# Strassen blocks of an attention, MoE and MLP kernel: order of the seven products, place of the rounded weight sums, and TensorE's order at the ends of the MLP's halves

## Chip, cores and metric

One core of one Trainium2 chip. The metric is the device time of one execution in microseconds (us), lower is better. Every execution computes attention, a mixture of experts and an MLP for the same inputs.

## What is computed

The reference, cut to what matters (2 batches of 8 heads, 576 positions, 64 per head; so 1152 tokens of 512):

```python
scores = q @ k.T / 8 + decay                 # decay from cumsum(log f), causal mask
x = softmax(scores) @ v                      # heads side by side: 1152 x 512
p = domain_probs / domain_probs.sum(-1)      # 1152 x 4
moe = sum(p[:, e:e+1] * (relu(x @ w1[e]) @ w2[e]) for e in range(4))   # 512 -> 1024 -> 512
h = moe @ w_in                               # 512 -> 2048
out = (h * sigmoid(1.702 * h)) @ w_out       # 2048 -> 512
```

## The kernel before

**Blocks and visits.** The four experts are worked as eight half experts, the MLP as four blocks: twelve blocks of 512 hidden columns, and a block's columns are four groups of 128. A block meets its tokens in visits. Visits 0 to 6 run beside the attention. Visits 7, 8 and 9 (`v_exp` to `v_all - 1`, the "early Strassen blocks") work two chunks of 320 tokens each, visits 10 to 13 the remaining MoE half experts (chunks of 320, 320 and 512 tokens), visit 14 (`v_mlp`) the first MLP block in the plain way, visits 15 to 17 the three other MLP blocks (three chunks of 384).

**Three matmuls for one.** Every operand is held as a rounded part and the rest of it (`xh`, `xl` for tokens, `whi`, `wlo` for weights, `hh`, `hl` for the hidden layer), and a product is hi·hi + lo·hi + hi·lo. ScalarE (ACT) rounds, VectorE (DVE) subtracts to get the rest.

**The joint first layer.** `emit_joint` (L869 on) works two chunks against two column groups at a time with seven products in place of eight (the Strassen scheme in Winograd's form). A visit has two such halves, m = 0 (groups 0 and 1) and m = 1 (groups 2 and 3). One product is six matmuls (L885). With the tokens' sums `th`, `tl` and the weights' sums `sh`, `sl`, the products are: into `pa` a11, into `pb` the second sum, into `pc` the first sum ("S1 product"), into `pd` the third ("S3 product"), into `pa` on top a12, into `pe` a22, and into `pc` on top the fourth ("S4 product"). Between them the outputs are combined: `u2 = pa` (ACT), `u2 = pb + u2` (DVE, L930), `u3 = pd + u2` (L914, in `third`), then one output each from `pc + u3` (L891, still in `third`), `u3 - pe` (`fourth`), and `pc + u2` after the S4 product (`fifth`). The output `pc + u3` has to be read before the S4 product adds to `pc`. In a MoE block an output goes from `pc` or `pe` to a buffer `jc`, in the MLP it is written over an accumulator, hence "DVE m L891" there. The plain output of `pa` goes through `evac_l1`: rounded by ACT, its rest by DVE (L963 in a MoE block, L966 in the MLP). In the second halves of visits 7 to 9 (`late_sums`) the a22 product stands second rather than sixth, since the sums are still being made.

**Sums.** POOL adds the raw weights (`sum_weights`), `split_sums` rounds them in two pieces of 512: ACT (L60, `sh<-sr`), DVE (L267, `sl<-sr,sh`), ACT, DVE. There is one buffer of sums: a new rounding may begin only when the S4 product of the half before has read the old one.

**Accumulators.** `ps_tile` (L122) hands out the eight PSUM buffers in turn; a product into a buffer waits until its last user has been read out. The second layer (`l2_products`, L972) uses the same buffers, read out by L1005 (MoE) or L1011 (MLP). In visits 7 to 9 the first half's columns (k 0 and 1) are worked for five token tiles before k 2 and 3. The plain first layer is L847.

**What sets the order.** A scheduler orders instructions by a simulated time line. DVE, ACT and POOL are held to source order from visit 7 on by `pin_turn` (L1097), TensorE (PE) only in visits 7 to 9:

```python
if v_ >= v_exp:
    (pin_engines.add if v_ < v_all else pin_engines.discard)(nc.tensor.engine)
    pin_turn()
```

In the MLP, DVE also converts weights (L342 to L357, `cvt`, `cvd`, `wf`) and makes their low parts (L230), in its fixed order between the steps of the halves. The main loop (L1170 on) emits a step's matmuls, then the work of the step before (`evac[0]()`), then what `place` has put at this step.

## Time and profile before

| | |
|---|---|
| median of 3 runs | 697.5 us (697.33 to 700.41) |
| profiled execution, its own time | 696.63 us |
| its span | 694.9 us |
| granted TensorE clock, mean | 1.00 |
| busy: PE, DVE, ACT, POOL | 98%, 72%, 49%, 32% |

The span is the time between the first and the last instruction; 1.73 us of the execution lie around it. A line of a waits view says which engine and line waited for which, how long in total, how often, and the longest. A row of a time line has the start, the busy time, engine, line, operation, out<-in, shapes and count, and in brackets the idle time before it and what ended it. A matmul's own time there is longer than its distance to the next, since matmuls overlap; distances are between starts.

### The profile page before, as it was taken

The page shows a single profiled execution, that of the slowest core. Times are in us where ns is not written, and L with a number is a line of the kernel's source. Part 1 is how long each engine was busy: PE and PEld are TensorE (multiplying, and loading weights), DVE is VectorE, ACT ScalarE, POOL GpSimd, SP SyncE. Part 2 cuts the span into 40 slices and gives each one's busy share as a digit, 9 for nine tenths or more (in the row PEclk, how much of TensorE's full clock was granted, in tenths as well). Part 3 has the DMA queues.
Part 4 walks back from the last instruction along what each step waited for, and adds up shares of the span by engine and source line. Part 5 has one row for each costly group of instructions (what it writes and reads, how often), then busy time and mean ns, then how long its engine had stood idle before and what let it go on. Part 6 is the DMA issues. An engine that isn't in the chain of part 4 may idle for free.

```text
span 694.9 us, 10725 instructions
## 1 busy us (share of the span) xinstructions
PE 683.6 (98%) x3828; PEld 596.3 (86%) x3829; DVE 502.1 (72%) x1057; ACT 342.1 (49%) x789; POOL 221.2 (32%) x266
## 2 busy tenths in 40 slices
PE   8999999999999999999999999999999999999997
PEld 4797888888988888888888888888899998988986
DVE  6896777666468677566966976788678779678632
ACT  5778767676532635634243344244446354434420
POOL 6887577532132454413214115112002302100000
PEclk9999999999999999999999999999999999999999
DMA  7786735423302034141423433444130343231012
GB/s 245 237 301 243 270 97 215 126 93 90 111 14 91 31 122 145 40 149 47 152 85 113 152 121 106 122 152 149 48 107 19 133 152 121 83 116 61 1 46 91
DMA packets 38597, 83.37 MB, mean 120 GB/s; under 512 B 3560, under 2 KB 3568, under 8 KB 38544
## 3 DMA queue, kind: packets, MB, share of 16 engines
q1 hardware_dynamic: 38504, 82.65, 36.0%
q8 instruction: 30, 0.49, 0.3%
q14 instruction: 23, 0.19, 0.1%
q10 hardware_dynamic: 40, 0.04, 0.0%
HBM read 71.88 MB, written 10.78 MB: 119 GB/s over the span
## 4 chain that ended last, share of the span: by engine, by line
PE 93%; DVE 3%; POOL 1%; ACT 1%; issue 1%; DMA 1%; SPq 0%; POOLq 0%; DVEq 0%; ACTq 0%
PE m L972 42%; PE m L847 20%; PE m L885 17%; PE s L568 4%; PE x L672 4%; PE t L642 3%; PE m L1117 1%; DMA dpraw<-in_dp_dram 1%; POOL ks L494 0%; PE m L864 0%; POOL e L624 0%; PE t L716 0%; PE m L1033 0%; POOL qlo L512 0%; PE s L571 0%
## 5 line engine op out<-in xcount | busy, mean ns | idle before, releaser
L972 PE MATMUL m<-whi,hh 128*128 128x512 f32 x432 | 122.6, 393 | 0.7 <-ACT hh L60 0.7
L972 PE MATMUL m<-wlo,hh 128*128 128x512 f32 x432 | 119.4, 390 | 0.0
L972 PE MATMUL m<-whi,hl 128*128 128x512 f32 x432 | 118.9, 390 | 0.0
L230 DVE TENSOR_TENSOR wlo<-wst,whi 128x512 fp32r<-128x512 f32 x140 | 103.0, 751 | 4.9 <-ACT whi L60 4.3
L972 PEld LDWEIGHTS m<-wlo,hh 128*128 128x128 f32 x432 | 80.9, 188 | 17.0
L972 PEld LDWEIGHTS m<-whi,hl 128*128 128x128 f32 x432 | 80.8, 188 | 16.9
L60 ACT ACTIVATE whi<-wst 128x512 fp32r<-128x512 f32 x144 | 85.4, 625 | 15.1 <-DMA wst<-in_wa_moe_dram 6.7
L972 PEld LDWEIGHTS m<-whi,hh 128*128 128x128 f32 x432 | 79.3, 188 | 14.7 <-ACT hh L60 1.1
L895 POOL TENSOR_TENSOR hl<-jc,hh 128x320 fp32r<-128x320 f32 x42 | 37.0, 882 | 160.1 <-ACT hh L60 153.3
L893 ACT ACTIVATE jc<-jc 128x320 f32<-128x320 f32 x42 | 19.7, 470 | 105.2 <-DVE jc L891 105.2
L251 POOL TENSOR_TENSOR sr<-wst 128x256 f32<-128x256 f32 x20 | 19.5, 976 | 154.0 <-DVE tl L287 48.1
L847 PE MATMUL m<-xh,wlo 128*128 128x256 f32 (+2 forms) x304 | 64.5, 325 | 0.0
L847 PE MATMUL m<-xl,whi 128*128 128x256 f32 (+2 forms) x304 | 64.2, 326 | 0.0
L847 PE MATMUL m<-xh,whi 128*128 128x256 f32 (+2 forms) x304 | 64.0, 327 | 0.0
L624 POOL TENSOR_SCALAR e<-e,sm 128x128 f32<-128x128 f32 (+4 forms) x72 | 46.0, 651 | 54.5 <-DVE sm L622 27.5
L963 DVE SCALAR_TENSOR_TENSOR hl<-m,hh 128x384 fp32r<-128x384 f32 (+2 forms) x82 | 36.0, 439 | 30.4 <-ACT hh L962 29.9
L1005 DVE SCALAR_TENSOR_TENSOR acc<-m,dpn,acc 128x512 f32<-128x512 f32 x63 | 46.6, 744 | 11.4 <-PE m L972 11.4
L847 PEld LDWEIGHTS m<-xh,whi 128*128 128x128 f32 x304 | 50.4, 189 | 3.2
L847 PEld LDWEIGHTS m<-xh,wlo 128*128 128x128 f32 x304 | 50.6, 189 | 2.5
L847 PEld LDWEIGHTS m<-xl,whi 128*128 128x128 f32 x304 | 50.2, 189 | 2.6
L614 ACT ACTIVATE e<-e,mx 128x128 f32<-128x128 f32 (+4 forms) x72 | 41.6, 580 | 11.7 <-DVE mx L598 11.0
L966 DVE TENSOR_TENSOR hl<-m,hh 128x384 fp32r<-128x384 f32 x48 | 26.6, 555 | 28.0 <-ACT hh L60 28.0
(138 smaller groups left out, 1292.0 us busy)
## 6 DMA issues: line engine op xcount, KB each, us to landing
wst<-in_wa_moe_dram SPq DMA_DIRECT2D x28, 512.0 KB, 3.6
wst<-in_wb_moe_dram SPq DMA_DIRECT2D x28, 512.0 KB, 4.1
mst<-in_wa_mlp_dram SPq DMA_DIRECT2D x16, 512.0 KB, 4.0
wm<-wf SPq DMA_DIRECT2D x32, 256.0 KB, 3.4
mst<-in_wb_mlp_dram SPq DMA_DIRECT2D x16, 512.0 KB, 3.8
wst<-wm SPq DMA_DIRECT2D x16, 512.0 KB, 3.5
cb<-cumd SPq DMA_DIRECT2D x16, 256.0 KB, 3.6
qr<-in_qk_dram SPq DMA_DIRECT2D x8, 384.0 KB, 4.9
```

Of the source, the lines that this page charges most:

```text
L60: return nc.scalar.activation(out=out, in_=in_, func=AF.Copy)
L230: (nc.gpsimd if v_ == 0 and kind == 'a' and g < 4 else nc.vector).tensor_sub(lf, raw, f(hf))
L568: nc.tensor.matmul(pt[:, :z - a], lhsT=lr[i][0], rhs=lr[i][1], start=i == 0 and not (both and pt is not bank), stop=i == n - 1, skip_group ...
L614: nc.scalar.activation(out=e[:, off:off + w], in_=e[:, off:off + w], func=AF.Exp, scale=-1.0, bias=mx, accum_out=sm[:, 0, k:k + 1])
L624: nc.gpsimd.tensor_scalar(out=e[:, off:off + w], in0=e[:, off:off + w], scalar1=sm[:, 0, i:i + 1], scalar2=1.0, op0=ALU.mult, op1=ALU.mult)
L672: nc.tensor.matmul(pt[64 * g:64 * g + 64, o:n], lhsT=lhsT, rhs=rhs, start=i == 0, stop=i == nk - 1)
L847: nc.tensor.matmul(p[:, :n], lhsT=w[:, k, :], rhs=x[c][:, k, :], start=(j == 0 and k == 0), stop=(j == 2 and k == 3))
L885: nc.tensor.matmul(p[:, :WN], lhsT=w[a][:, k, :], rhs=x[z][:, k, :], start=start and j == 0 and k == 0, stop=stop and j == 2 and k == 1, s ...
L895: nc.gpsimd.tensor_sub(hl[:, g, :], r, f(hh[:, g, :]))
L963: nc.vector.scalar_tensor_tensor(out=l_, in0=q, scalar=0.0, in1=f(h_), op0=ALU.max, op1=ALU.subtract)
L972: nc.tensor.matmul(p, lhsT=h_tile(v_, b, c, j, x, k), rhs=wb[v_, k][w].rearrange("p a c -> p (a c)"), start=i == 0 and k == 0, stop=i == 2 ...
L1005: nc.vector.scalar_tensor_tensor(out=a, in0=p, scalar=d, in1=a, op0=ALU.mult, op1=ALU.add)
```

## The change

- In the second halves of visits 7 to 9 the S3 product goes ahead of the S1 product, `third` (u3) and `third_out` (the output that reads `pc`) become two steps, and the accumulators are taken in another turn: `pa`, `pc`, one left unused, `pe`, `pb`, `pd`.
- In every MoE joint half the plain output's two operations are taken apart: `plain_out` (ACT) where they were, `plain_low` (DVE) after the `fourth` output.
- Sums of the next visit: `split_sums` at its two places is replaced by `high_sums` (both ACT roundings) ahead of the previous step's outputs and `low_sums` (both DVE subtractions) behind them; likewise for the second half of visit 7.
- In the main loop PE is held to source order also in visits 15 to 17: in the second half and in the first two steps of the plain first layer behind it.

```diff
@@ -260,11 +260,30 @@
     def split_sums(*at):
         if at or sum_due:
             v_, m, raw = (*at, placed_sums.pop(at)) if at else sum_due.pop(0)
-            sh, sl = ws[v_, m] = tuple(late["ws"].tile([128, 4, 2, 128], F32R, tag=t, name=t) for t in ("sh", "sl"))
-            hs, ls = (t.rearrange("p s k c -> p (s k c)") for t in (sh, sl))
+            hs, ls = begin_sums(v_, m)
             for o in (0, 512):
                 round_act(hs[:, o:o + 512], raw[:, o:o + 512])
                 nc.vector.tensor_sub(ls[:, o:o + 512], raw[:, o:o + 512], f(hs[:, o:o + 512]))
+
+    def begin_sums(v_, m):
+        ws[v_, m] = tuple(late["ws"].tile([128, 4, 2, 128], F32R, tag=t, name=t) for t in ("sh", "sl"))
+        return tuple(t.rearrange("p s k c -> p (s k c)") for t in ws[v_, m])
+
+    def high_sums(v_, m):
+
+        raw = placed_sums.pop((v_, m)) if v_ in placed else sum_due.pop(0)[2]
+        hs, ls = begin_sums(v_, m)
+        for o in (0, 512):
+            round_act(hs[:, o:o + 512], raw[:, o:o + 512])
+        low_due[v_, m] = raw, hs, ls
+
+    def low_sums(v_, m):
+
+        raw, hs, ls = low_due.pop((v_, m))
+        for o in (0, 512):
+            nc.vector.tensor_sub(ls[:, o:o + 512], raw[:, o:o + 512], f(hs[:, o:o + 512]))
+
+    low_due = {}
 
     sum_due = []
 
@@ -901,51 +920,74 @@
             a11, a12 = (tuple(t[:, k:k + 2] for t in wa[v_, g]) for k in (0, 2))
             a22 = tuple(t[:, 2:4] for t in wa[v_, g2])
             s1, s2, s3, s4 = (tuple(t[:, i] for t in ws[v_, m]) for i in range(4))
-            pa, pb, pc = (ps_tile() for _ in range(3))
+            if late_sums:
+                pa, pc, _, pe, pb, pd = (ps_tile() for _ in range(6))
+            else:
+                pa, pb, pc = (ps_tile() for _ in range(3))
             u = []
 
             def first_part():
                 u.extend(tmp_p.tile([128, WMAX], F32, tag="tmp", name=n)[:, :WN] for n in ("u2", "u3"))
                 nc.scalar.activation(out=u[0], in_=pa[:, :WN], func=AF.Copy)
 
-            pd, pe = [], []
+            def second():
+                nc.vector.tensor_add(u[0], pb[:, :WN], u[0])
 
             def third():
-                nc.vector.tensor_add(u[1], pd[0][:, :WN], u[0])
-                output(c2, g2, nc.vector.tensor_add, pc, u[1], pd[0])
+                nc.vector.tensor_add(u[1], pd[:, :WN], u[0])
+
+            def third_out():
+                output(c2, g2, nc.vector.tensor_add, pc, u[1], pd)
 
             def fourth():
-                output(c1, g2, nc.vector.tensor_sub, pe[0], u[1], pe[0])
+                output(c1, g2, nc.vector.tensor_sub, pe, u[1], pe)
 
             def fifth():
                 output(c2, g, nc.vector.tensor_add, pc, u[0], pc)
+
+            def both_(*parts):
+                return lambda: [q() for q in parts]
+
+            hh, hl = h_of(v_, b, c1)[0][2]
+            plain_hi, plain_lo = hh[:, g, :], hl[:, g, :]
+
+            def plain_out():
+                if b < NMOE:
+                    nc.scalar.activation(out=plain_hi, in_=pa[:, :WN], func=AF.Relu)
+                else:
+                    evac_l1(v_, b, c1, g, pa)
+
+            def plain_low():
+                if b < NMOE:
+                    nc.vector.scalar_tensor_tensor(out=plain_lo, in0=pa[:, :WN], scalar=0.0, in1=f(plain_hi),
+                                                   op0=ALU.max, op1=ALU.subtract)
 
             product(pa, a11, ts[11], True, True)
             yield first_part
             if late_sums:
-                pe.append(ps_tile())
-                product(pe[0], a22, ts[4], True, True)
+                product(pe, a22, ts[4], True, True)
                 yield lambda: None
-            product(pb, s2, ts[2], True, True)
-            yield lambda: nc.vector.tensor_add(u[0], pb[:, :WN], u[0])
-            product(pc, s1, ts[1], True, True)
-            yield lambda: None
-            pd.append(ps_tile())
-            product(pd[0], s3, ts[3], True, True)
-            if late_sums:
-                def two():
-                    third()
-                    fourth()
-
-                yield two
+                product(pb, s2, ts[2], True, True)
+                yield second
+                product(pd, s3, ts[3], True, True)
+                yield third
+                product(pc, s1, ts[1], True, True)
+                yield both_(third_out, fourth)
+                product(pa, a12, ts[21], False, True)
+                yield both_(plain_out, plain_low)
             else:
-                yield third
-            product(pa, a12, ts[21], False, True)
-            yield lambda: evac_l1(v_, b, c1, g, pa)
-            if not late_sums:
-                pe.append(ps_tile())
-                product(pe[0], a22, ts[4], True, True)
-                yield fourth
+                product(pb, s2, ts[2], True, True)
+                yield second
+                product(pc, s1, ts[1], True, True)
+                yield lambda: None
+                pd = ps_tile()
+                product(pd, s3, ts[3], True, True)
+                yield both_(third, third_out)
+                product(pa, a12, ts[21], False, True)
+                yield plain_out
+                pe = ps_tile()
+                product(pe, a22, ts[4], True, True)
+                yield both_(fourth, plain_low)
             product(pc, s4, ts[22], False, True)
             yield fifth
 
@@ -1155,12 +1197,14 @@
             h0, h1, l2 = (3, v_, b, c1), (3, v_, b, c2), (4, v_, b, c1)
             put(h0, 1, sum_weights, v_ + 1, 0)
             put(h1, 1, sum_weights, v_ + 1, 1)
-            put(l2, 0, split_sums, v_ + 1, 0)
-            put((5, v_, b, c1), 0, split_sums, v_ + 1, 1)
+            for u, m in ((l2, 0), ((5, v_, b, c1), 1)):
+                put(u, -1, high_sums, v_ + 1, m)
+                put(u, 0, low_sums, v_ + 1, m)
             first = v_ == v_exp
             places = [(h1, 5), (h1, 6)] + [(l2, i) for i in range(1, 7)]
             if first:
-                put((6,) + units[-1], 0, split_sums_done)
+                put((6,) + units[-1], -1, high_sums, v_, 1)
+                put((6,) + units[-1], 0, low_sums, v_, 1)
                 nxt0 = (3, v_ + 1, visits[v_ + 1][0], c1)
                 places = [(h0, 0), (h0, 1)] + places + [(nxt0, 0), (nxt0, 1)]
             todo = [("b", v_)] * first + [("a", v_ + 1), ("b", v_ + 1)]
@@ -1232,6 +1276,9 @@
                 if d[0] == 0:
                     split_due.remove(d)
                     rests.append(split_output(d[1]))
+            if g == 0:
+                for what, args in place_at.get((u, -1), ()):
+                    what(*args)
             evac[0]()
             for r in rests:
                 r()
@@ -1257,7 +1304,8 @@
                     cv_due[0] -= 1
                 load_owed()
             if v_ >= v_exp:
-                (pin_engines.add if v_ < v_all else pin_engines.discard)(nc.tensor.engine)
+                end = v_ > v_mlp and (kind == 3 and m == 1 or kind == 1 and g < 2)
+                (pin_engines.add if v_ < v_all or end else pin_engines.discard)(nc.tensor.engine)
                 pin_turn()
             else:
                 pin_from[1] = len(nc.cur_bb.bb.instructions)
```

How the instructions move, on PE (rows: line, operation, out<-in with the tiles' numbers, shape, count; `x` the tokens, `t` their sums, `s` the weights' sums, `w` weights). First, visit 8, second half. Before, from the S1 product (m_3435 is `pc`), then S3 (m_3471), a12 (m_3433) and S4:

```order
L885 MATMUL m_3435<-th_2881,sh_3420 128x320 x2
L885 MATMUL m_3435<-th_2881,sl_3421 128x320 x2
L885 MATMUL m_3435<-tl_2882,sh_3420 128x320 x2
L885 MATMUL m_3471<-th_2881,sh_3420 128x320 x2
L885 MATMUL m_3471<-th_2881,sl_3421 128x320 x2
L885 MATMUL m_3471<-tl_2882,sh_3420 128x320 x2
L885 MATMUL m_3433<-xh_77,whi_3280 128x320 x2
L885 MATMUL m_3433<-xh_77,wlo_3281 128x320 x2
L885 MATMUL m_3433<-xl_78,whi_3280 128x320 x2
L885 MATMUL m_3435<-xh_77,sh_3420 128x320 x2
L885 MATMUL m_3435<-xh_77,sl_3421 128x320 x2
L885 MATMUL m_3435<-xl_78,sh_3420 128x320 x2
```

Now, from the S3 product (m_3439), then S1 (m_3435 is `pc` again), a12 and S4:

```order
L904 MATMUL m_3439<-th_2881,sh_3416 128x320 x2
L904 MATMUL m_3439<-th_2881,sl_3417 128x320 x2
L904 MATMUL m_3439<-tl_2882,sh_3416 128x320 x2
L904 MATMUL m_3435<-th_2881,sh_3416 128x320 x2
L904 MATMUL m_3435<-th_2881,sl_3417 128x320 x2
L904 MATMUL m_3435<-tl_2882,sh_3416 128x320 x2
L904 MATMUL m_3434<-xh_77,whi_3281 128x320 x2
L904 MATMUL m_3434<-xh_77,wlo_3282 128x320 x2
L904 MATMUL m_3434<-xl_78,whi_3281 128x320 x2
L904 MATMUL m_3435<-xh_77,sh_3416 128x320 x2
L904 MATMUL m_3435<-xh_77,sl_3417 128x320 x2
L904 MATMUL m_3435<-xl_78,sh_3416 128x320 x2
```

S1 and S3 have changed places: `pd` is complete one product sooner, and between the end of `pc`'s S1 product and S4 there is one product (a12) where there were two.

Second, visit 10, between its two halves. Before, from the S4 product of the first half (m_3893) to the first row of the second half that reads new sums (sh_3979); the plain first layer (L847) lies between:

```order
L885 MATMUL m_3893<-xh_77,sh_3800 128x320 x2
L885 MATMUL m_3893<-xh_77,sl_3801 128x320 x2
L885 MATMUL m_3893<-xl_78,sh_3800 128x320 x2
L847 MATMUL m_4089<-xh_77,wlo_3785 128x512
L847 MATMUL m_4089<-xl_78,whi_3784 128x512 x4
L847 MATMUL m_4110<-xh_77,whi_3813 128x512 x4
L847 MATMUL m_4110<-xh_77,wlo_3814 128x512 x4
L847 MATMUL m_4110<-xl_78,whi_3813 128x512 x4
L885 MATMUL m_3993<-th_2881,sh_3979 128x320 x2
```

Now:

```order
L904 MATMUL m_3995<-xh_77,whi_3816 128x320 x2
L904 MATMUL m_3995<-xh_77,wlo_3817 128x320 x2
L904 MATMUL m_3995<-xl_78,whi_3816 128x320 x2
L904 MATMUL m_3896<-xh_77,sh_3797 128x320 x2
L904 MATMUL m_3896<-xh_77,sl_3798 128x320 x2
L904 MATMUL m_3896<-xl_78,sh_3797 128x320 x2
L904 MATMUL m_3996<-th_2881,sh_3977 128x320 x2
L904 MATMUL m_3997<-th_2881,sh_3977 128x320 x2
L904 MATMUL m_4023<-th_2881,sh_3977 128x320 x2
```

The sums' products of the second half (sh_3977) follow directly on the S4 product of the first (sh_3797).

Third, visit 16, the end of its second half. Before, the plain first layer of the third chunk stands ahead of the S4 product (m_6728):

```order
L847 MATMUL m_6858<-xh_77,whi_6457 128x384 x4
L847 MATMUL m_6858<-xh_77,wlo_6458 128x384 x4
L847 MATMUL m_6858<-xl_78,whi_6457 128x384 x4
L847 MATMUL m_6887<-xh_77,whi_6488 128x384 x4
L847 MATMUL m_6887<-xh_77,wlo_6489 128x384 x4
L847 MATMUL m_6887<-xl_78,whi_6488 128x384 x4
L885 MATMUL m_6728<-xh_77,sh_6675 128x384 x2
L885 MATMUL m_6728<-xh_77,sl_6676 128x384 x2
L885 MATMUL m_6728<-xl_78,sh_6675 128x384 x2
L972 MATMUL m_6913<-whi_6736,hh2_2861 128x512
```

Now, from the a22 product (m_6801) on, S4 is m_6731:

```order
L904 MATMUL m_6801<-th_2881,whi_6491 128x384 x2
L904 MATMUL m_6801<-th_2881,wlo_6492 128x384 x2
L904 MATMUL m_6801<-tl_2882,whi_6491 128x384 x2
L904 MATMUL m_6731<-xh_77,sh_6678 128x384 x2
L904 MATMUL m_6731<-xh_77,sl_6679 128x384 x2
L904 MATMUL m_6731<-xl_78,sh_6678 128x384 x2
L866 MATMUL m_6823<-xh_77,whi_6407 128x384 x4
L866 MATMUL m_6823<-xh_77,wlo_6408 128x384 x4
L866 MATMUL m_6823<-xl_78,whi_6407 128x384 x4
L866 MATMUL m_6841<-xh_77,whi_6430 128x384 x4
```

The S4 product stands right behind the sixth product, ahead of the 48 matmuls of the plain first layer. In visit 15 it moves the same way, with two second-layer matmuls left between; in visit 17 it moves to the same place. The S4 product of visit 16's first half moves too: it now stands 15 second-layer matmuls further ahead. The rows of DVE, ACT and POOL in visits 15 to 17 stand as before.

## Rows read from the trace of the kernel before

**Rows 1.** The page: busy time by engine; the chain that ended last, by engine.

```profile
PE 683.6 (98%) x3828; PEld 596.3 (86%) x3829; DVE 502.1 (72%) x1057; ACT 342.1 (49%) x789; POOL 221.2 (32%) x266
...
PE 93%; DVE 3%; POOL 1%; ACT 1%; issue 1%; DMA 1%; SPq 0%; POOLq 0%; DVEq 0%; ACTq 0%
```

**Rows 2.** Waits of PE: total us, times, longest us.

```profile
PE m L885 <- DVE jc L891: 0.9, 3, 0.3
...
PE m L885 <- DVE acc L1005: 0.7, 2, 0.4
PE m L972 <- ACT hh L60: 0.7, 1, 0.7
```

**Rows 3.** Time line of PE, visit 8, second half: S3 product, S4 product.

```profile
256.70 0.46 PE L885 MATMUL m<-tl,sh 128*128 128x320 f32 x2
257.50 0.56 PE L885 MATMUL m<-th,sh 128*128 128x320 f32 x2 [0.34 <-DVE acc L1005]
257.90 0.45 PE L885 MATMUL m<-th,sl 128*128 128x320 f32 x2
258.19 0.46 PE L885 MATMUL m<-tl,sh 128*128 128x320 f32 x2
...
260.70 0.56 PE L885 MATMUL m<-xh,sh 128*128 128x320 f32 x2 [0.30 <-DVE jc L891]
```

**Rows 4.** Time line of DVE and of ACT, the same half.

```profile
256.71 1.40 DVE L1005 SCALAR_TENSOR_TENSOR acc<-m,dpn,acc 128x512 f32<-128x512 f32 x2
...
259.56 0.49 DVE L914 TENSOR_TENSOR u<-m,u 128x320 f32<-128x320 f32 x1 [1.06 <-PE m L885]
260.16 0.49 DVE L891 TENSOR_TENSOR jc<-m,u 128x320 f32<-128x320 f32 x1
...
254.58 1.14 ACT L60 ACTIVATE sh<-sr 128x512 fp32r<-128x512 f32 x2
```

**Rows 5.** Time line of PE and of ACT and DVE, visit 16, first half's end.

```profile
600.01 0.51 PE L885 MATMUL m<-xh,sh 128*128 128x384 f32 x2
...
601.07 0.63 PE L972 MATMUL m<-wlo,hh 128*128 128x512 f32 x2
601.53 1.09 PE L972 MATMUL m<-whi,hl 128*128 128x512 f32 x4
...
601.33 1.15 ACT L60 ACTIVATE sh<-sr 128x512 fp32r<-128x512 f32 x2 [2.97 <-PE m L885]
...
601.99 1.29 DVE L267 TENSOR_TENSOR sl<-sr,sh 128x512 fp32r<-128x512 f32 x2 [3.04 <-ACT sh L60]
```

**Rows 6.** Time line of DVE and of PE, visit 12, first half.

```profile
390.06 0.75 DVE L1005 SCALAR_TENSOR_TENSOR acc<-m,dpn,acc 128x512 f32<-128x512 f32 x1
...
390.80 0.46 PE L885 MATMUL m<-xh,whi 128*128 128x320 f32 x2
```

**Rows 7.** Visit 15, second half: PE, DVE; then busy times of a stretch.

```profile
554.91 0.51 PE L885 MATMUL m<-xh,whi 128*128 128x384 f32 x2
...
568.63 0.51 PE L885 MATMUL m<-xh,sh 128*128 128x384 f32 x2
...
564.19 0.57 DVE L891 TENSOR_TENSOR m<-m,u 128x384 f32<-128x384 f32 x1
...
556.13:564.75 8.62, 8.62 (x52) 8.62 (x51) 8.44 (x15) 4.46 (x9) 1.47 (x2) 1.00 0.40 127
```

(The last row's columns: the stretch, its length, then PE, PEld, DVE, ACT and POOL busy with counts, granted clock, DMA share, GB/s.)

**Rows 8.** Visit 16, second half: PE from its seven products on, DVE, busy times.

```profile
602.46 0.51 PE L885 MATMUL m<-xh,whi 128*128 128x384 f32 x2
...
608.71 0.85 PE L847 MATMUL m<-xh,whi 128*128 128x384 f32 x4
...
615.16 0.57 DVE L891 TENSOR_TENSOR m<-m,u 128x384 f32<-128x384 f32 x1
...
601.99:615.73 13.74, 13.74 (x80) 13.64 (x79) 12.53 (x22) 5.17 (x10) 3.20 (x4) 1.00 0.34 113
```

**Rows 9.** Visit 17, second half: PE behind six products, DVE.

```profile
657.27 0.85 PE L847 MATMUL m<-xh,whi 128*128 128x384 f32 x4
...
655.98 0.57 DVE L891 TENSOR_TENSOR m<-m,u 128x384 f32<-128x384 f32 x1
```

**Rows 10.** Busy times of the last stretch, behind the last matmul (columns as before).

```profile
691.40:694.90 3.50, 0.00 (x0) 0.00 (x0) 0.65 (x1) 0.00 (x0) 0.00 (x0) 1.00 0.19 75
```

## The prediction

> **What bounds the kernel now.** I read the page first: TensorE is busy 98% of the span, and 93% of the chain that ended last lies on it [rows 1]. So the end is set by TensorE's work, which the change leaves alone, and by the few places where TensorE stands still. What a change of order is worth is counted there: each us in which TensorE waits no longer is a us of the end, each us of new waiting is one more. DVE, at 72%, costs only where TensorE comes to it too early.
>
> Then the waits of TensorE. Three kinds belong to the changed code: three waits of the joint layer for DVE's `jc` (0.9 us together), two for the second layer's read-out (0.7), and one wait of the second layer for ACT's `hh` (0.7) [rows 2]. The time line of visit 8's second half shows what such a wait costs in all [rows 3]. Pairs of matmuls follow each other at 0.29 us (257.90 to 258.19). Across the wait for L1005 it is 0.80 us (256.70 to 257.50), and the first pair behind it takes 0.40: 0.51 + 0.11 = 0.62 lost where the idle time printed is 0.34. A wait costs its idle time and about 0.27 us for getting going again.
>
> **The change, part by part.** Sums are made against the profiled execution, 696.63 us: its span of 694.9 us and 1.73 us around it. The median of the runs, 697.5, is 0.9 us above it; I move the median by the same difference.
>
> *S3 ahead of S1, `third` in two, other accumulators, roundings first (visits 7 to 9).* The S4 product waits because DVE reads `pc` last: in visit 8 `u3` starts at 259.56, the output behind it at 260.16 and ends at 260.65, and S4 starts at 260.70 with 0.30 idle before [rows 3, 4]. Now `pd` is complete one product earlier, `u3` is done while S1 runs, and one DVE operation of 0.49 us stands between `pc` and S4, against the six matmuls of a12 (6 x 0.147 = 0.88). A pair's busy time is 0.17 us longer than its distance to the next (0.46 against 0.29 [rows 3]), and with that taken off 0.2 us are to spare. The wait for L1005 (visits 8 and 9) falls because `pc` takes a buffer that is read out earlier, and because DVE's two read-outs (1.40 us from 256.71) no longer stand behind the low sums [rows 4]. Gain: five waits, 0.9 + 0.7 = 1.6 us idle [rows 2] and 5 x 0.27 = 1.35 for getting going: 2.9 us. Bounds: 1.6 (only what is printed as idle) to 3.0. I take **-2.9**, as the spacing of the rows shows the whole.
>
> What pays for it is hidden. The roundings, 1.14 us of ACT [rows 4], now stand ahead of the last outputs of a half, which so come 1.1 us later; their readers in the second layer (k 2 and 3) stand behind five token tiles on k 0 and 1, 30 matmuls at 0.23 us (six of them from 601.07 to 602.46 [rows 5, 8]), 6.9 us. Without that cover it would cost 1.1 us a half. The plain output's low part, moved behind the next output, comes later by one DVE operation, 0.5 us, under the same cover.
>
> *Visit 10.* Its S4 product of the first half is now followed directly by products that read the new sums, which can be rounded only when S4 has read the old ones; 17 matmuls used to lie between. No row shows this wait; the same step in visit 16 does: S4's six matmuls start from 600.01 on, and the next matmul at 601.07; ACT's first rounding starts at 601.33 and DVE's first low sums at 601.99 [rows 5]. The pairs that read the first rounded sums may start when the first of the two roundings is done, which is where DVE starts: 601.99 - 601.07 = 0.9. Bounds 0.3 (601.33 - 601.07, if only the start of the rounding counted) and 2.2 (until DVE's subtractions end, 601.99 + 1.29). I take **+0.9**.
>
> *Visits 11 to 13.* The a22 product moves ahead of a12 in the first half and needs a buffer that L1005 empties: in visit 12 from 390.06 to 390.81, while the product could start at 390.80 [rows 6]. 0 to +0.5; I take **0**.
>
> *Visit 15, second half.* The first six products start at 554.91; 36 matmuls at 0.174 (6.25 us between 602.46 and 608.71 for the same 36 [rows 8]) end them at 561.16, and two second-layer matmuls at 561.6. Now S4 stands there. But it must wait for the output that reads `pc`, and DVE gets to it at 564.19 and ends it at 564.75 [rows 7]. DVE does not idle on the way: between 556.13 and 564.75 it is busy 8.44 of 8.62 us with 15 operations, weight conversions and low parts among them, in an order that the change leaves alone [rows 7]. Before, S4 came at 568.63 behind 43 plain first-layer matmuls and met nothing. New wait: 564.75 - 561.6 = **+3.2** (2.9 to 3.5).
>
> *Visit 16.* The first half's S4 moves ahead of 15 second-layer matmuls, from 600.01 to 596.56 (15 x 0.23 = 3.45). ACT's rounding had idled 2.97 us for it and DVE 3.04 behind that [rows 5], so DVE's queue moves up by 3.0 us. In the second half the six products end at 608.71 as before, where the plain first layer stood [rows 8]. Now S4 stands there, and its output on DVE ended at 615.16 + 0.57 = 615.73; less 3.0 that is 612.7. New wait: 612.7 - 608.7 = **+4.0**. Lower bound 3.0, if DVE loses less; upper 7.0, if none of the 3.0 us reaches the output, since DVE was busy 12.53 of 13.74 us on the way [rows 8] and parts of that are fed by transfers. I stay with 4.0: the whole queue stood behind that idle time. In exchange the wait of L972 for `hh` [rows 2], with its getting going, goes: **-1.0**, as `hh` is finished from S4 while 48 matmuls run.
>
> *Visit 17.* Six products end at 657.27, the output on DVE at 655.98 + 0.57 = 656.55 [rows 9]: **0**.
>
> Sum: -2.9 + 0.9 + 0 + 3.2 + 4.0 - 1.0 + 0 = **+4.2 us**. The profiled execution would take 700.8 us, the median 697.5 + 4.2 = **701.7 us**. Nothing later takes the waits in again: behind visit 15 TensorE has work without a gap but for the wait counted away.
>
> **The rivals.** *The clock falls in a wait.* The granted clock was 1.00 in every stretch that I read, and also between 691.40 and 694.90, 3.5 us with no matmul at all [rows 10]; but no matmul follows there that would show a slower clock, and no wait of TensorE in the MLP is that long today. [...] Chance 0.13. [...]
>
> *Only one of the two MLP waits appears.* If DVE were through in visit 16 by 608.7, the sum would be +0.2 (697.7 us); if in visit 15 by 561.6, +1.0 (698.5). For it: TensorE's waiting in visit 15 gives DVE 3.2 us in which it needn't keep up. Against it: DVE's order is fixed, its conversions in visit 16 stand behind outputs of that visit, and it would have to save 4.0 of 12.5 busy us. Time 698.1, chance 0.18.
>
> *Faster: DVE is in time in both.* Then S4 in source order costs nothing, and only the gains stay: -2.9 - 1.0 = -3.9, with visit 10's wait between 0 and 0.9: 693.6 to 694.5 us. It needs the output 3.2 us sooner in visit 15 and 4.0 sooner in visit 16; that point decides. For it speaks only visit 17, where the same order is in time by 0.7 us [rows 9]. Against it stands the busy DVE of [rows 7, 8]. Chance 0.12.
>
> *The change doesn't do what it says* in the early blocks: the one DVE operation behind `pc` isn't covered, since 0.2 us is little; then three waits stay at up to 0.57 and the sum is +4.2 + 1.7 = +5.9. I leave it in the forecast's range.
>
> **How the numbers follow.** Forecast 0.57, clock 0.13, one wait 0.18, none 0.12. About 0.5%, 3.5 us, is what a measurement of this kernel tells from no change: 694.0 to 701.0 counts as the same. The forecast with its bounds runs from 700 to 704, and as 701.7 is near the border I put 0.45 of its 0.57 above it. Slower: 0.45 + 0.13 = 0.58. Same: 0.12 + 0.18 + 0.05 of the last case = 0.35. Faster: 0.07. The range leaves out the last case and the tail of the clock case: 698.0 to 705.0.
>
> **What the trace would show.** Right: no wait of the joint layer for `jc` or L1005 in visits 7 to 9; two waits of the joint layer for "DVE m L891", some 3 and 4 us long, from about 560 and 610 on (561.6 and 608.7, moved by the terms before), just ahead of the S4 pairs; one of about 0.9 us behind visit 10's first S4, for ACT's `sh`; none for `hh` in the second layer of visit 16; granted clock 1.00. Wrong: if the MLP's S4 pairs start within 0.5 us of the sixth product, or DVE's rows there end 3 us sooner than I moved them, or the clock falls behind a wait.

## The result and the profile after

The changed kernel takes 704.4 us (median of 5 runs, 703.42 to 705.32) against 697.33 us before: ratio 1.0099, 95% interval 1.0085 to 1.0112, so 7.1 us slower, where +4.2 was forecast and 705.0 was the upper end of the range. The profiled execution took 704.96 us, its span is 703.2 us against 694.9, its mean granted clock 0.992 against 1.00.

The waits of TensorE (PE) after the change, sorted by their totals (line, what it waited for, us in all, times, longest):

```profile
PE m L904 <- DVE m L910: 5.6, 2, 3.5
...
PE m L904 <- ACT sh L60: 0.7, 1, 0.7
PE m L1014 <- DVE u L934: 0.5, 1, 0.5
```

L904 is the joint product (L885 before), L1014 the second layer (L972), L910 the output that reads `pc` (L891). The three kinds of waits that the change was read against [rows 2] are gone. In their place stand two waits for the output in the MLP, 5.6 us together, one for `sh` (visit 10), and one for `u`, which belongs to visit 15 as well.

Visit 8's second half, where TensorE waited twice [rows 3], on PE's time line:

```profile
257.47 0.46 PE L904 MATMUL m<-tl,sh 128*128 128x320 f32 x2
257.77 0.46 PE L904 MATMUL m<-th,sh 128*128 128x320 f32 x2
...
259.23 0.46 PE L904 MATMUL m<-xl,whi 128*128 128x320 f32 x2
259.53 0.48 PE L904 MATMUL m<-xh,sh 128*128 128x320 f32 x2
```

In [rows 3] the pair at 257.50, which waited for the buffer, begins the S1 product into `pc` (S3 follows it at 258.48). S1 now starts at 257.77, and pairs follow at 0.30 us across both places: no wait for the buffer there, none for the output at 259.53. On DVE's time line the read-outs are over at 255.82, 1.95 us before S1 needs its buffer, and the output from `pc` is done at 259.39, 0.14 us before S4:

```profile
254.42 1.40 DVE L1047 SCALAR_TENSOR_TENSOR acc<-m,dpn,acc 128x512 f32<-128x512 f32 x2
...
258.90 0.49 DVE L910 TENSOR_TENSOR jc<-m,u 128x320 f32<-128x320 f32 x1 [0.44 <-PE m L904]
```

From visit 7's first S4 to the last pair of visit 9's last S4, 61.72 us have become 58.73, 3.0 less (PE's time line, before, then after):

```profile
226.97 0.45 PE L885 MATMUL m<-xh,sh 128*128 128x320 f32 x2
288.69 0.45 PE L885 MATMUL m<-xl,sh 128*128 128x320 f32 x2
```

```profile
227.39 0.45 PE L904 MATMUL m<-xh,sh 128*128 128x320 f32 x2
286.12 0.45 PE L904 MATMUL m<-xl,sh 128*128 128x320 f32 x2
```

Visit 10, between the halves, where S4 of the first half is now followed directly by products that read the new sums:

```profile
306.83 0.46 PE L904 MATMUL m<-xl,sh 128*128 128x320 f32 x2
308.00 0.71 PE L904 MATMUL m<-th,sh 128*128 128x320 f32 x3 [0.72 <-ACT sh L60]
```

From start to start 1.17 us in place of 0.29: 0.88 lost, the 0.9 of the forecast.

The second halves of visits 15 and 16 on PE's time line, one after the other:

```profile
559.28 0.51 PE L904 MATMUL m<-tl,whi 128*128 128x384 f32 x2
560.28 0.73 PE L1014 MATMUL m<-whi,hh 128*128 128x512 f32 x2 [0.48 <-DVE u L934]
563.15 1.01 PE L904 MATMUL m<-xh,sh 128*128 128x384 f32 x2 [2.14 <-DVE m L910]
563.96 0.84 PE L904 MATMUL m<-xh,sl 128*128 128x384 f32 x2
564.60 0.84 PE L904 MATMUL m<-xl,sh 128*128 128x384 f32 x2
...
611.46 0.51 PE L904 MATMUL m<-tl,whi 128*128 128x384 f32 x2
...
615.43 1.01 PE L904 MATMUL m<-xh,sh 128*128 128x384 f32 x2 [3.46 <-DVE m L910]
616.23 0.84 PE L904 MATMUL m<-xh,sl 128*128 128x384 f32 x2
616.87 0.84 PE L904 MATMUL m<-xl,sh 128*128 128x384 f32 x2
...
621.16 0.86 PE L866 MATMUL m<-xh,whi 128*128 128x384 f32 x4
621.86 0.85 PE L866 MATMUL m<-xh,wlo 128*128 128x384 f32 x4
```

Two things are to be seen. S4 waits as it was read from the trace of before: in visit 15 from 559.28 to 563.15 there are 3.87 us, less 0.35 for the last pair of a22 and 0.46 for two second-layer matmuls: 3.1 lost. In visit 16 it is 3.97 - 0.35 = 3.6. And behind each wait a pair takes 0.64 us to the next (563.96 to 564.60, 616.23 to 616.87), where 0.35 is usual (0.70 for four matmuls, 621.16 to 621.86). The stretches from S4's start on, of the windows view (length; PE, PEld, DVE, ACT, POOL busy with counts; granted clock; DMA share; GB/s), tell why:

```profile
563.15:572.00 8.85, 8.85 (x43) 8.85 (x44) 5.71 (x12) 5.66 (x13) 0.00 (x0) 0.82 0.51 175
615.43:627.40 11.97, 11.97 (x54) 11.97 (x55) 8.55 (x17) 8.46 (x19) 0.00 (x0) 0.77 0.14 47
```

The granted clock is 0.82 and 0.77 there, the only such stretches of the MLP: it falls before each wait is over and is still down for some us behind it (in the same view 0.50 from 563.00 to 566.00 and from 614.50 to 620.00, but 1.00 from 572.00 to 600.00 and from 627.40 on). The second stretch holds the six S4 and the 48 plain matmuls, 9.4 us at 0.174 each; they take 11.97. That is 2.6 us for the clock; in the first stretch 8.85 x 0.18 = 1.6.

So the difference is: -3.0 (early blocks), +0.9 (visit 10), +3.1 and +1.6 (visit 15), +3.6 and +2.6 (visit 16), -1.0 (the wait for `hh`, gone), together +7.8, beside +8.3 between the two profiled executions and +7.1 between the medians. Another 0.4 us between the profiled executions lies ahead of visit 7's first S4 (226.97 to 227.39). The profiled execution is also 0.6 us slower than its median; the five executions run from 703.42 us at a mean clock of 0.995 to 705.32 at 0.992.

### The profile page after: what moved, and what is told of

It is laid out like the page before. It is cut to its first block, busy times and chain, and to the rows that moved or that the text cites. A ratio compares the mean times of both kernels' runs of the same rounds, so it can differ in the third digit from the quotient of the medians.

```text
span 703.2 us, 10725 instructions
## 1 busy us (share of the span) xinstructions
PE 687.7 (98%) x3828; PEld 600.4 (85%) x3829; DVE 504.8 (72%) x1057; ACT 342.1 (49%) x789; POOL 222.3 (32%) x266
## 4 chain that ended last, share of the span: by engine, by line
PE 90%; DVE 4%; ACT 2%; DMA 2%; POOL 1%; issue 1%; SPq 0%; ACTq 0%; POOLq 0%
PE m L1014 41%; PE m L866 20%; PE m L904 17%; PE s L587 4%; PE x L691 3%; PE t L661 2%; DMA wst<-in_wa_moe_dram 2%; ACT e L633 1%; PE m L1159 1%; DMA dpraw<-in_dp_dram 1%; DVE cvd L374 0%; ACT whi L60 0%; PE m L883 0%; DVE sl L266 0%; PE t L735 0%
## 5 line engine op out<-in xcount | busy, mean ns | idle before, releaser
L1014 PE MATMUL m<-whi,hh 128*128 128x512 f32 x432 | 121.9, 392 | 0.5 <-DVE u L934 0.5
L1014 PE MATMUL m<-wlo,hh 128*128 128x512 f32 x432 | 119.4, 390 | 0.0
L1014 PE MATMUL m<-whi,hl 128*128 128x512 f32 x432 | 118.7, 390 | 0.0
L230 DVE TENSOR_TENSOR wlo<-wst,whi 128x512 fp32r<-128x512 f32 x140 | 105.1, 766 | 5.4 <-ACT whi L60 4.9
L1014 PEld LDWEIGHTS m<-wlo,hh 128*128 128x128 f32 x432 | 80.9, 188 | 16.9
L1014 PEld LDWEIGHTS m<-whi,hl 128*128 128x128 f32 x432 | 80.9, 188 | 16.9
L1014 PEld LDWEIGHTS m<-whi,hh 128*128 128x128 f32 x432 | 79.3, 188 | 14.4 <-DVE u L934 0.8
L914 POOL TENSOR_TENSOR hl<-jc,hh 128x320 fp32r<-128x320 f32 x42 | 39.1, 933 | 160.0 <-ACT hh L60 153.6
L1047 DVE SCALAR_TENSOR_TENSOR acc<-m,dpn,acc 128x512 f32<-128x512 f32 x63 | 46.6, 744 | 12.5 <-PE m L1014 12.5
L633 ACT ACTIVATE e<-e,mx 128x128 f32<-128x128 f32 (+4 forms) x72 | 41.7, 581 | 11.7 <-DVE mx L617 11.2
L999 ACT ACTIVATE m<-m 128x384 f32<-128x384 f32 x48 | 23.1, 480 | 42.2 <-DVE m L910 41.0
```

What stands on the lines that cost most here:

```text
L230: (nc.gpsimd if v_ == 0 and kind == 'a' and g < 4 else nc.vector).tensor_sub(lf, raw, f(hf))
L633: nc.scalar.activation(out=e[:, off:off + w], in_=e[:, off:off + w], func=AF.Exp, scale=-1.0, bias=mx, accum_out=sm[:, 0, k:k + 1])
L914: nc.gpsimd.tensor_sub(hl[:, g, :], r, f(hh[:, g, :]))
L999: nc.scalar.activation(out=p[:, :n], in_=p[:, :n], func=AF.Gelu_apprx_sigmoid)
L1014: nc.tensor.matmul(p, lhsT=h_tile(v_, b, c, j, x, k), rhs=wb[v_, k][w].rearrange("p a c -> p (a c)"), start=i == 0 and k == 0, stop=i == 2 ...
L1047: nc.vector.scalar_tensor_tensor(out=a, in0=p, scalar=d, in1=a, op0=ALU.mult, op1=ALU.add)
```

## The experiments

All were run beside the kernel before, whose median was 697.3 to 697.5 us in each comparison.

**early_only: the change without source order in the MLP.**

```diff
-                end = v_ > v_mlp and (kind == 3 and m == 1 or kind == 1 and g < 2)
+                end = False
```

> The change without its last part: TensorE is not held to source order in the MLP, so the S4 products of visits 15 and 16 stand behind the plain first layer again. Theory (the early blocks gain 3.0 us, visit 10 costs 0.9, the two waits in the MLP and the slower clock behind them make all the rest): 697.3 - 3.0 + 0.9 = 695.2 us, no wait for DVE's L910 in the MLP, clock 1.00. Rival (the new order in the early blocks shifts work elsewhere and is itself part of the loss): 698 us or more.

Measured: 694.79 us, ratio 0.9960 (0.9947 to 0.9973), clock 0.999, no wait for L910 in the MLP. Its waits of PE that belong to the changed code:

```profile
PE m L904 <- ACT sh L60: 0.7, 1, 0.7
PE m L1014 <- ACT hh L60: 0.7, 1, 0.7
```

The first is visit 10's, the second visit 16's old one [rows 2], back again. The early blocks gain, and source order in the MLP costs 704.4 - 694.8 = 9.6 us.

**pin_15 and pin_16: source order in one visit alone.** `v_ > v_mlp and` becomes `v_ == v_mlp + 1 and` or `v_ == v_mlp + 2 and`.

> The change with source order in visit 15 alone. Theory (wait of 3.0 us for the output on DVE, then matmuls at half clock for 1.8 us more): 695.2 + 4.8 = 700.0 us. Rival (a wait alone, the clock falls only because both waits come): 695.2 + 3.0 = 698.2 us, clock 1.00.

Measured: 698.21 us (1.0015, 1.0003 to 1.0027), 3.4 above early_only. That is the rival's number, but not its reason: the wait is there and the clock falls.

```profile
PE m L904 <- DVE m L910: 2.1, 1, 2.1
```

```profile
555.00:575.00 20.00, 17.37 (x86) 16.17 (x86) 16.27 (x31) 12.56 (x27) 0.14 (x1) 0.91 0.43 133
```

The clock of 0.91 over 20 us is 20 x 0.09 = 1.8 us, near the 1.6 of the changed kernel. What the theory had left out is that the wait for `hh` in visit 16 goes with this wait: its row is absent here. 3.1 + 1.6 - 1.0 = 3.7. The median hides a spread: the twelve executions run from 697.53 to 700.66 us, at mean clocks from 1.00 down to 0.995 (the profiled one: 697.92 us, 0.997), while the 17 executions of the kernel before in that comparison stay at 0.998 or more. That suggests that the clock does not fall alike behind this wait in every execution; only one of them has a trace.

> The change with source order in visit 16 alone; the S4 product of that visit's first half then keeps its late place, so DVE does not get its 3.0 us. Theory (wait 7.0 us instead of 3.6, about 2.7 us of slow clock behind it, 1.0 us of waiting for hh saved): 695.2 + 7.0 + 2.7 - 1.0 = 703.9 us. Rivals: wait as in the changed kernel, since DVE's start does not hang on that S4 product: 695.2 + 3.6 + 2.7 - 1.0 = 700.5 us; the clock's cost grows with the wait: 705 us or more.

Measured: 703.32 us (1.0081, 1.0068 to 1.0094), the theory's 703.9. PE's time line:

```profile
613.77 1.01 PE L904 MATMUL m<-xh,sh 128*128 128x384 f32 x2 [6.90 <-DVE m L910]
...
619.43 0.85 PE L866 MATMUL m<-xh,whi 128*128 128x384 f32 x4
```

With the first half's S4 in its late place the wait is 6.9 us, so DVE's start does hang on that S4. From 613.77 to 619.43 stand 6 + 12 = 18 matmuls, 5.66 us in place of 18 x 0.174 = 3.1: the slow clock costs 2.5 us behind a wait of 6.9, no more than the 2.6 behind one of 3.5.

**fill: matmuls that nobody needs, in the waits.**

```diff
+            for i in range({v_mlp + 1: 12, v_mlp + 2: 18}.get(v_, 0) * m):
+                nc.tensor.matmul(pb[:, :WN], lhsT=a11[0][:, i % 2, :], rhs=ts[11][0][:, i % 2, :], start=True, stop=True,
+                                 skip_group_check=True)
             product(pc, s4, ts[22], False, True)
```

> The changed kernel with extra matmuls, whose results nobody reads, ahead of the S4 product of visits 15 (12 of them) and 16 (18), about as long as the waits. Theory (the clock falls because TensorE stands still, 1.8 us lost in visit 15 and 2.7 in visit 16): clock 1.00, 704.4 - 4.5 = 699.9 us, DVE's output where it was. Rival (the clock falls for another reason, or the slow matmuls wait for DVE or for weights): 704 us or more, since the extra work ends before DVE is done.

Measured: 701.11 us (1.0048, 1.0035 to 1.0060), 3.3 under the changed kernel. PE's time line in visit 16, and the stretch around it:

```profile
610.41 0.51 PE L904 MATMUL m<-tl,whi 128*128 128x384 f32 x2
611.17 3.42 PE L992 MATMUL m<-xh,whi 128*128 128x384 f32 x18 [0.25 <-DVE u L934]
614.43 0.57 PE L904 MATMUL m<-xh,sh 128*128 128x384 f32 x2
614.83 0.52 PE L904 MATMUL m<-xh,sl 128*128 128x384 f32 x2
```

```profile
610.00:622.00 12.00, 11.75 (x68) 11.32 (x67) 8.77 (x18) 4.20 (x10) 0.00 (x0) 1.00 0.31 111
```

S4 starts 4.02 us after the last a22 pair, as in the changed kernel (3.97), so nothing is gained there; but the clock stays at 1.00, and from the first pair of S4 to the next it is 0.40 us where it was 0.80. That the clock falls because TensorE stands still is shown, with its price: 3.3 us by the medians, against the 4.5 that were put in and the 4.2 that the stretches gave. The traces place most of the rest: from the first product of visit 15's second half to the end of the span the changed kernel takes 149.95 us (from 553.25) and this one 146.08 (from 553.62), 3.9 less, with S4 up to 0.1 us later in each visit. And the median execution of the changed kernel, 0.6 us below the profiled one, has the higher mean clock, 0.993 against 0.992.

**pin_only: source order in the MLP alone, on the kernel before.** The `end` line of the change, nothing else.

> The kernel before, with source order in the MLP as in the change and nothing else of it. Here the scheduler puts other plain first-layer products, which are not held, ahead of S4: 24 in visit 15 (4.2 us) and 12 in visit 16 (2.1 us), and visit 16's first S4 stays late. Theory (wait = DVE's lateness less what TensorE has to do first): none in visit 15; in visit 16 7.0 - 2.1 = 4.9 us, slow clock 2.4, hh wait saved 1.0: 697.3 + 6.3 = 703.6 us. Rival (source order costs the same here as in the changed kernel, 704.4 - 694.8 = 9.6): 706.9 us.

Measured: 703.06 us (1.0082, 1.0068 to 1.0096). The total is near the theory's, partly by luck, and the place is not the theory's: in visit 16 TensorE waits at a plain product (L847) that stands ahead of S4 and needs a buffer which DVE's `u2` empties (L930), behind the same queue of DVE.

```profile
614.15 0.96 PE L847 MATMUL m<-xh,whi 128*128 128x384 f32 x4 [3.71 <-DVE u L930]
614.95 0.98 PE L847 MATMUL m<-xh,wlo 128*128 128x384 f32 x4
615.73 1.48 PE L847 MATMUL m<-xl,whi 128*128 128x384 f32 x4
```

From the first product of visit 15's second half to the end of the span it is 139.99 us before (from 554.91) and 144.82 here (from 556.48): 4.8 us, where the theory has 6.3. The rest of the 6.4 between the profiled executions lies ahead of visit 15, and its cause isn't shown. So other work ahead of S4 covers a wait only if it has a free buffer; in visit 15 it had one, and no wait shows there.

**hold, hold_unpinned and hold2: DVE's conversions out of the way.** In hold, none run in the second halves, and at most two steps per step behind them:

```diff
-                while cv_due[0] >= 1:
+                if v_ > v_mlp:
+                    n = 0 if kind == 3 and m == 1 else 2
+                else:
+                    n = 99
+                while cv_due[0] >= 1 and n > 0:
                     in_turn(next, cv_gen[0], None)
                     cv_due[0] -= 1
+                    n -= 1
```

> The changed kernel, with the weight conversions (L362 to L376) not run during the second halves of visits 15 to 17 but behind them, at most two steps of them per step of the main loop. Theory (S4 waits because DVE works 4.9 and 5.6 us of conversions ahead of the output it needs): no wait of the joint layer for L910 in the MLP, clock 1.00, and the wait for hh gone too: 694.8 - 1.0 = 693.8 us. Rival (DVE is late because its outputs follow the products by their own chain, or the conversions, run later, come too late for the next weights): waits of 2 us or more stay or come elsewhere, 697 us or more.

Measured: 701.09 us (1.0054, 1.0042 to 1.0067); the expectation was missed by 7 us. PE's time line in visits 15 and 16:

```profile
561.22 0.62 PE L904 MATMUL m<-xh,sh 128*128 128x384 f32 x2 [1.22 <-DVE m L910]
...
612.36 1.01 PE L904 MATMUL m<-xh,sh 128*128 128x384 f32 x2 [3.75 <-DVE m L910]
```

In visit 15 the wait shrank from 2.14 us idle to 1.22, and no pair behind it is slow:

```profile
558.00:570.00 12.00, 10.78 (x61) 10.35 (x60) 8.74 (x17) 6.92 (x16) 0.00 (x0) 1.00 0.46 152
```

Five conversions stand ahead of the output there instead of eight, with the first half's S4 at its place in the change. The output ends 9.85 us behind the half's first product (553.25) in the change and 8.19 behind it (552.98) here, 1.7 us sooner; of the 3.1 us lost, 1.4 are left (DVE's time line of the change, then of hold):

```profile
562.53 0.57 DVE L910 TENSOR_TENSOR m<-m,u 128x384 f32<-128x384 f32 x1
```

```profile
560.60 0.57 DVE L910 TENSOR_TENSOR m<-m,u 128x384 f32<-128x384 f32 x1
```

In visit 16 the wait is as long as ever. The edit had not done what I meant: the steps between the two halves still ran conversions, and DVE's time line of visit 16 has six of them ahead of the output, from 603.43 to 608.3; the first is

```profile
603.43 0.74 DVE L374 SCALAR_TENSOR_TENSOR cvd<-mst,cvt 128x512 f32<-128x512 uint32 x1
```

Besides, in visit 16 the scheduler put the first half's S4 eight second-layer matmuls later than in the change, so DVE's chain began later.

> The same holding back, with TensorE not held to source order in the MLP (as in the run early_only). Theory (S4 stands behind the plain first layer there and waits for nothing, so an earlier output is worth nothing; only the wait for hh in visit 16 could go): 693.8 to 694.8 us. Rival (source order has a worth of its own once DVE is in time): 1 us or more above the run hold.

Measured: 693.55 us (0.9946, 0.9933 to 0.9958). No wait for `hh` in visit 16, and of the changed code's waits only visit 10's is left (one of 0.4 us for a rounded weight is new). The rival's sign is refuted: without source order the same kernel is 7.5 us faster than hold.

hold2 holds the conversions over both halves and the steps between, and lets four run per step afterwards:

```diff
+    before_units = {seq[i - 1] for i, q in enumerate(seq) if q[0] == 3 and q[1] > v_mlp and q[3] == MLP[1]}
...
+                n = 99 if v_ < v_mlp else 0 if kind == 3 or u in before_units else 4
```

> The changed kernel with TensorE in source order, and no weight conversion at all between the first half of visits 15 to 17 and the output that S4 waits for: they are held back over both halves and the steps between, then run at most four to a step. In the run hold six of them still stood ahead of that output in visit 16. Theory (S4 waits exactly for DVE's work ahead of the output): both waits at most 0.5 us, clock 1.00, hh wait gone: 693.8 to 694.8 us. Rival (the output follows from the half's own chain, or conversions then come too late and TensorE waits for weights): 697 us or more.

Measured: 699.51 us (1.0023, 1.0011 to 1.0036). Half right. Visit 15 comes out as expected: on PE's time line S4 follows without a wait, DVE's output having ended at 559.0:

```profile
559.73 0.63 PE L1014 MATMUL m<-whi,hh 128*128 128x512 f32 x2
560.19 0.52 PE L904 MATMUL m<-xh,sh 128*128 128x384 f32 x2
```

But two things have changed there. The conversions are gone from ahead of the output, and the scheduler has put the first half's S4 eight second-layer matmuls sooner than in the change, so that the sums' low parts start 3.4 us ahead of the second half instead of 1.6. Of the 4.3 us by which the output comes sooner, that is 1.8. So the conversions are the larger part of visit 15's wait (in hold, where S4 stands as in the change, three of them are 1.7 us); that they are the whole of it isn't shown. In visit 16 2.44 us idle remain, and the clock falls behind them (0.87 from 611.20 to 624.00; PE's time line):

```profile
611.20 0.62 PE L904 MATMUL m<-xh,sh 128*128 128x384 f32 x2 [2.44 <-DVE m L910]
611.66 0.51 PE L904 MATMUL m<-xh,sl 128*128 128x384 f32 x2
612.00 0.74 PE L904 MATMUL m<-xl,sh 128*128 128x384 f32 x2
612.54 1.49 PE L866 MATMUL m<-xh,whi 128*128 128x384 f32 x4
```

DVE has no conversion there, but its chain begins late (DVE's time line):

```profile
602.62 1.29 DVE L266 TENSOR_TENSOR sl<-sr,sh 128x512 fp32r<-128x512 f32 x2 [3.74 <-ACT sh L60]
...
610.58 0.57 DVE L910 TENSOR_TENSOR m<-m,u 128x384 f32<-128x384 f32 x1
```

The scheduler had moved the first half's S4 behind the first four matmuls of the second half (600.65). From the sums to the output DVE needs 8.5 us with no conversion at all (read-outs of the second layer and three low parts stand between); TensorE, from the first sums' product at 602.64 to the end of a22, six. So in visit 16 S4 in source order meets a late output either way: by conversions, or by the first S4's place. A version with both moved was not tried.

**The pieces of the early blocks: no_turn, old_round, pin_10.** All without source order in the MLP. no_turn takes the accumulators one after the other:

```diff
-                pa, pc, _, pe, pb, pd = (ps_tile() for _ in range(6))
+                pa, pe, pb, pc, pd = (ps_tile() for _ in range(5))
```

> As early_only, but the accumulators of the late halves are taken one after the other, without the buffer left unused. Theory (the waits for L1005 go because DVE's read-outs no longer stand behind the low sums; the turn only shifts every later buffer, and with it the scheduler's order in visit 10, where the 0.9 us come from): no wait for ACT's sh in visit 10, none for L1047 or for jc in visits 7 to 9: 694.8 - 0.9 = 693.9 us. Rival (the turn is what removes the waits for the read-out): two waits of 0.6 us back, 693.9 + 1.2 = 695.1 us.

Measured: 693.69 us (0.9944, 0.9931 to 0.9958): the theory, to 0.2 us. No wait for L1047, none for `jc`, none for `sh` in visit 10. The other turn isn't needed, and it is what brings visit 10's 0.9 us: it shifts the buffers behind it, and the scheduler orders visit 10 differently.

old_round splits the sums as before:

```diff
-            for u, m in ((l2, 0), ((5, v_, b, c1), 1)):
-                put(u, -1, high_sums, v_ + 1, m)
-                put(u, 0, low_sums, v_ + 1, m)
+            put(l2, 0, split_sums, v_ + 1, 0)
+            put((5, v_, b, c1), 0, split_sums, v_ + 1, 1)
```

> As early_only, but the sums are split as before (rounding, subtraction, rounding, subtraction, behind the previous step's outputs). Theory (the roundings' place matters, since with it the read-outs stand behind the low sums again and the sums come 1 us later): a wait of 0.5 us or more in each of visits 8 and 9, 695.9 us. Rival (order of S3 and turn do it all, the place of the roundings is worth nothing): 694.8 us.

Measured: 697.41 us (1.0003, 0.9991 to 1.0015), 2.6 us above early_only; the roundings' place is worth that, but not where I expected it. PE's waits show no read-out, but one of 0.4 us for `jc` and, on PE's time line, this:

```profile
309.77 1.15 PE L904 MATMUL m<-th,sh 128*128 128x320 f32 x6 [2.17 <-ACT sh L60]
```

Visit 10's wait grows from 0.72 to 2.17 us idle, since ACT's rounding stands behind the outputs there. The waits for the read-out (two on PE before) are gone here, without the roundings' new place, and in no_turn, without the unused buffer: neither of the two is needed by itself. Both runs keep S3 ahead of S1, which also changes which product takes which buffer, and that was not tried alone. The three waits for `jc`, 0.9 us idle and about 1.7 with their getting going, are gone in both as well (the one of 0.4 us in old_round is in visit 9's first half), so they are put down to S3 ahead of S1 and the split of `third`; this is argued, not shown.

> As early_only (no source order in the MLP), with TensorE held to source order in visit 10. Theory (the 0.9 us behind visit 10's first S4 product come from the scheduler placing it directly ahead of the products that read the new sums; source order puts 16 second-layer rows between): 694.8 - 0.9 = 693.9 us. Rival (S4, being earlier, waits for its own output on DVE instead): 694.8 us or more, with a wait for L910 in visit 10.

Measured: 694.68 us (0.9959, 0.9946 to 0.9971): the rival. One wait is traded for another:

```profile
PE m L904 <- DVE jc L910: 0.6, 1, 0.6
```

**early_and_hold: the pieces that paid.** no_turn and hold's edit, without source order in the MLP.

> The pieces that paid, together: S3 ahead of S1 and the roundings first, accumulators in the plain turn (no_turn), TensorE not held to source order in the MLP, and conversions held back as in hold_unpinned. Theory (the two gains touch different places: visit 10's wait of 0.9 us and visit 16's wait for hh of 0.9 us): 693.7 - 0.9 = 692.8 us, no wait of TensorE over 0.3 us after 200 us. Rival (the order that the scheduler finds in the MLP hangs on the buffers' turn, so that holding back does not remove the hh wait here): 693.7 us.

Measured: 692.68 us (0.9930, 0.9917 to 0.9944), as expected, 4.7 us faster than before and 11.7 faster than the change. PE's waits there:

```profile
PE m L1075 <- DVE acc L1068: 1.9, 1, 1.9
```

It and the others, of 0.9 us and less, belong to the attention at the start. Of the changed code nothing over 0.3 us is left.

## Why the prediction was right and where it failed

*Early blocks, -2.9.* Right in size and cause: five waits gone, 3.0 us. Two reasons were given for the waits on the read-out; they are gone without the one (old_round) and without the unused buffer of the other (no_turn), so the accumulators' new turn was not needed.

*Visit 10, +0.9.* Right: 0.88 in the trace, 1.1 by the medians of early_only and no_turn (694.8 - 693.7). The price taken from visit 16's first S4 [rows 5] was the right row.

*Visits 11 to 13 and 17, 0.* Right; no wait shows there.

*Visit 15, +3.2.* Measured 3.1. The cause as given, DVE's fixed order with conversions ahead of the output [rows 7], is shown for 1.7 us by hold; hold2 ends the wait, but with the first half's S4 moved too.

*Visit 16, +4.0 - 1.0.* Measured 3.6, and the wait for `hh` gone. The output came 3.45 us sooner against the products (3.57 us behind a22's end, 7.02 before), as far as the 15 matmuls by which S4 moved; 3.0 had been taken. That DVE's queue moves up because the first S4 does is shown by pin_16, where that S4 stays late and 6.9 us are waited: the 7.0 given as the upper bound. That the wait for `hh` would fall was put down to this visit's own order; in pin_15 and hold_unpinned it falls without that.

*The clock: the step that failed.* The waits alone come to +3.6 (-3.0 + 0.9 + 3.1 + 3.6 - 1.0), close to the +4.2. The other 4.2 us are the clock. It stood in the prediction as a rival with chance 0.13. It fell in both of the new waits, to 0.50, and cost 1.6 and 2.6 us: it belonged in the sum, once for each wait, and not beside it. What I allowed for it, in the chance and in the upper end of the range, was my estimate: no trace that I had read by then showed a slower clock. The row that I held against it was no evidence, as the prediction itself says: a stretch without a matmul behind it can't show a slow one [rows 10]. fill shows the cause: S4 starts no sooner, but TensorE works until then, the clock stays at 1.00 and at least 3.3 us come back. Behind 6.9 us of waiting the price was 2.5, behind 3.46 us 2.6, so it doesn't follow the wait. That 704.4 us lies inside 698.0 to 705.0 is luck: the forecast's own bounds ended at 704, its trace was to show a clock of 1.00, and the range reached higher only for the rivals' sake.

The other rivals fell: neither MLP output came in time, and no wait for `jc` stayed in visits 7 to 9, though the 0.2 us to spare were 0.14 in visit 8.

## What to carry to other kernels

A matmul that must not overwrite what another engine still has to read should stand where that engine has got to in its own order, not where the source has it: the scheduler's 48 matmuls ahead of S4 were the cover for it. When a change makes TensorE stand still for some us where it ran without a gap, count the wait and a second term for the slow clock that may come behind it (1.5 to 2.6 us here, where it came). And a turn of buffers is no local edit: the new turn with its unused buffer cost 0.9 us in the next visit here.

## What the runs showed of the hardware

In the profiled executions the clock fell with waits of 2.14 us idle (with one of 0.48 shortly ahead of it; changed kernel, 0.82 from 563.15 to 572.00), 2.44 (hold2, 0.87 from 611.20 to 624.00), 3.46 (changed kernel, 0.77 from 615.43 to 627.40), 3.71 (pin_only, 0.93 from 605.00 to 630.00), 3.75 (hold, 0.86 from 612.00 to 624.00) and 6.90 us (pin_16, 0.80 from 605.00 to 630.00) in the MLP. It did not fall behind the one of 1.22 us in hold (1.00 from 558.00 to 570.00), nor behind the one of 2.17 us in visit 10 of old_round (windows view, from the end of that wait):

```profile
309.77:320.00 10.23, 10.23 (x56) 9.20 (x57) 7.42 (x14) 2.64 (x7) 1.25 (x2) 1.00 0.23 77
```

So among these waits of about 2 us, 2.14 and 2.17, the idle time alone does not tell. Where I worked the price out, it was of one size, 1.5 to 2.6 us: 1.6 behind 2.14 us, 1.5 behind 3.75 (hold, 612.00 to 624.00: 58 matmuls in 11.64 us, 10.1 at 0.174 each), 2.6 behind 3.46 and 2.5 behind 6.90.

How soon the slow matmuls come differs too. After 3.46 us the first pair is slow already (0.80 us to the next in the changed kernel, 0.40 in fill). In hold2, after 2.44 us, the first pairs of S4 still follow at 0.46 and 0.34 us and only later matmuls are slow (1.28 us for four, 612.54 to 613.82). In pin_only, after 3.71 us, eight matmuls go by at about 0.2 us each before the slow ones (614.15 to 615.73). What the chip looks at to decide this the runs don't show.
